# Attention products in row halves and column strips, plain float32, with TensorE's order written out by hand

## The chip, the cores and the metric

The kernel runs on one core of one Trainium2 chip. The metric is the device time of one execution in microseconds. Five engines of the core work side by side, each on its own queue of instructions, in order: PE (TensorE, matrix products, with weight loads shown apart as PEld), DVE (VectorE), ACT (ScalarE), POOL (GpSimd) and SP (SyncE, which issues the DMAs here). They wait for each other through semaphores.

## The reference

A linear attention with exponential features, followed by a gated feed-forward. Sizes: batch 8, 8 heads, 576 positions, head size 64, 128 features; the feed-forward takes 4608 tokens of 512 through 1536 and back. All float32.

```python
def phi(x):
    proj = np.einsum('bhsd,df->bhsf', x, w_phi)
    proj = proj - np.max(np.abs(proj), axis=-1, keepdims=True)
    return np.concatenate([np.exp(proj), np.exp(-proj)], axis=-1)
q_p, k_p = (phi(q), phi(k))
kv = np.einsum('bhsf,bhsd->bhfd', k_p, v)
z = np.sum(k_p, axis=2)
num = np.einsum('bhsf,bhfd->bhsd', q_p, kv)
den = np.einsum('bhsf,bhf->bhs', q_p, z)[..., None] + 1e-06
attn = num / den            # then x: tokens x (heads * head size)
gate = 1.0 / (1.0 + np.exp(-(x @ w_gate)))
val = x @ w_val
out = gate * val @ w_out
```

## The kernel before

**Stages.** The attention goes over 32 pairs: 8 batches of 4 pairs of heads, two heads side by side in 128 partitions. The feed-forward's 1536 inner columns are 12 blocks of 128. Blocks 0 to 4 (`JA = 5`) run beside the attention, in chunks of 256 tokens, as soon as a batch has left its rows in the scratch `xscr`; their partial result goes to `yscr`. After the attention a second phase (`rest_chunks`) runs blocks 5 to 11 in chunks of 512 tokens, adds the partial result and writes the output. The change leaves the second phase as it is.

**A pair.** `att_q` projects q (product `pq`, lines 397 and 403), copies it to `d` and subtracts the largest absolute value, found by DVE over a transposed layout (lines 413 to 428). `att_k` projects k (`pk`, lines 316 and 321), takes maxima (line 325) and exponentials `ek` (line 338 straight from PSUM in the first `DIRECT` = 4 pairs, line 350 after a subtraction in the others), multiplies them with v, which carries a column of ones for the sum z (`kvp`, line 358: v's 65 columns are the weights, 256 features stream), copies the result (`kvt`, line 364) and transposes it in four pieces (`tp`, line 367). `att_num` takes the exponentials of q (`eq`, line 439) and multiplies (`nm`, line 456: 65 columns of weights, the last one the denominator, 288 positions stream). `att_norm` sends the denominator row through DRAM (`dn`, `den`, `rb`) to get reciprocals in all partitions, and `att_scale` multiplies (`xp`, line 484) and writes x.

**Number formats.** A product of plain float32 is two instructions on PE. In the feed-forward and in the attention's projections and numerators from pair 8 on, operands are split into two parts of type float32r (`split`: ACT rounds, DVE takes the rest), and a product becomes three cheaper ones (two for q, where both parts are stacked). The first `WHOLE` = 8 pairs, and `kvp` always, use plain float32.

**Order.** The order of every engine's instructions, PE's included, is worked out by the framework's planner from a simulated timeline and from priorities: attention steps are emitted under `attend` with a priority, and the feed-forward's units are let in by `fill`, called four times a pair, at 0.7 units a call:

```python
due = min(due + RATE, 2.0) if ready else 0.0
while ready and due >= 1.0:
    ready.pop(0)()
    due -= 1.0
```

A unit is a block of a chunk: `mm_in` (line 136) 24 products into `gv`, then `gated`; `half_out` makes the partial result (`mm_out`, line 143, into `acc`). Weights come as float64 words and are taken apart by DVE and ACT (`from_f64`), 15 such pieces while the first pairs run.

**PSUM.** Eight banks: two for `gv`, three for `pp` (pk and pq), one each for `kvp`/`tp`, `nm` and `acc`.

Of the kernel before, what the change touches and what calls it, by code (L numbers as in the profile page):

```python
# [31 lines left out]
KVW = D + 1  # L32
# [3 lines left out]
WHOLE = 8  # first pairs: plain float32 products, no splits  # L36
DIRECT = 4  # first pairs: K's exponentials straight from PSUM
PRIORITY = 400
RATE, LAG = 0.7, 2  # feed-forward units per slot; slots from x to its first unit
# [3 lines left out]
def attention_moe(  # L43
# [29 lines left out]
    def from_f64(h, l, raw, mid, sp, nb, name):  # L73
        # h: the value cut to 12 bits; l: the other bits as an integer times their unit
# [26 lines left out]
    def load_weights(j, m, wp, sp, nb, twice):  # L101
# [58 lines left out]
    def half_units(cs, js, mp, ps_gv, ps_acc):  # L160
# [11 lines left out]
        def unit(c, i):  # L172
            begin(c)
            n = f"1_{c}_{js[i]}"
            gv = ps_gv.tile([P, 2, CH], F32, tag="gv", name="gv" + n)
            for m in range(2):
                mm_in(gv[:, m, :], xs[c], js[i], m, CH)
            hs[c, i] = gated(gv[:, 0, :], gv[:, 1, :], CH, mp, 6, n)
            if i == 1:
                begin(c + 1, hs[c, i][2])  # L180
# [10 lines left out]
        for c in cs:  # L191
            for i in range(len(js)):
                items.append(lambda c=c, i=i: unit(c, i))
                if i == 0:
                    items += outs
            outs = [(lambda c=c, t=t: half_out(c, t)) for t in range(2)]
# [60 lines left out]
    with ExitStack() as actx:  # L257
# [10 lines left out]
        ident = at1.tile([KVW, KVW], F32, name="ident")  # L268
        make_identity(nc, ident)
        wk = at1.tile([P, 3 * F], F32, name="wk")  # L270
        nc.sync.dma_start(wk, w_phi)
        wq = at1.tile([P, 2, 3 * F], F32R, name="wq")
        split(wq[:, 0, :], wq[:, 1, :], wk)
# [3 lines left out]
        loaded, kvs, qst, marks = {}, {}, {}, []  # L277
        rbs, late = {}, {}

        def load_q(b, p):  # L280
            qx = at.tile([P, S], F32, tag="qin", name=f"q{b}_{p}")
            nc.sync.dma_start(qx, q[b, p])
            loaded["q", b, p] = qx

        def load_kv(b, p):
# [3 lines left out]
            vx = at.tile([P, 10, KVW], F32, tag="vin", name="v" + n)  # L289
            nc.sync.dma_start(vx, v[b, p])  # L290
            loaded["kv", b, p] = (kx, vx)

        def att_k(b, p):
            n = f"{b}_{p}"
            kx, vx = loaded.pop(("kv", b, p))
            kvp = ps_kv.tile([KVW, 2, 2 * F], F32, tag="kvp", name="kvp" + n)
            es = []
            whole = b * NP + p < WHOLE
            if not whole:
                kh = at.tile([P, 4 * P], F32R, tag="kh", name="kh" + n, bufs=2)  # L300
                kl = at.tile([P, 4 * P], F32R, tag="kl", name="kl" + n, bufs=2)
                split(kh, kl, kx[:, : 4 * P])
            for g in range(3):
                pp = ps_p.tile([P, 4, F], F32, tag="pp", name=f"pk{n}_{g}")
                if g < 2:
                    ns = 4
                    for i in range(2):
                        o = pp[:, 2 * i : 2 * i + 2, :].rearrange("p a f -> p (a f)")
                        ts = slice((2 * g + i) * P, (2 * g + i + 1) * P)
                        terms = [(kx, wk[:, : 2 * F])] if whole else [  # L310
                            (kh, wq[:, 0, : 2 * F]),
                            (kh, wq[:, 1, : 2 * F]),
                            (kl, wq[:, 0, : 2 * F]),
                        ]
                        for t, (x, w) in enumerate(terms):
                            nc.tensor.matmul(  # L316
                                o, x[:, ts], w, start=t == 0, stop=t == len(terms) - 1
                            )
                else:
                    ns = 1  # L320
                    nc.tensor.matmul(
                        pp[:, 0, :], kx[:, 4 * P :], wk[:, 2 * F :], start=True, stop=True
                    )
                mx = at.tile([P, 4], F32, tag="mx", name=f"mx{n}_{g}")
                vec.tensor_reduce(
                    mx[:, :ns], pp[:, :ns, :], axis=AX.X, op=ALU.max,
                    apply_absolute_value=True,
                )
                e = at.tile(
                    [P, ns, 2 * F], F32, tag=f"ek{ns}", name=f"ek{n}_{g}",  # L330
                    bufs=2 if ns > 1 else 2,
                )
                if b * NP + p < DIRECT:
                    mn = at.tile([P, 4], F32, tag="mn", name=f"mn{n}_{g}")
                    vec.tensor_scalar(mn[:, :ns], mx[:, :ns], -1.0, None, op0=ALU.mult)
                    for i in range(ns):
                        for sg in (1, 0):
                            act.activation(  # L338
                                e[:, i, sg * F : sg * F + F], pp[:, i, :], AF.Exp,
                                bias=(mn, mx)[sg][:, i : i + 1], scale=1.0 - 2.0 * sg,  # L340
                            )
                else:
                    dk = at.tile([P, ns, F], F32, tag=f"dk{ns}", name=f"dk{n}_{g}")
                    vec.tensor_tensor(
                        dk, pp[:, :ns, :],
                        mx[:, :ns].unsqueeze(2).broadcast_to([P, ns, F]),
                        op=ALU.subtract,
                    )
                    for sg in range(2):
                        act.activation(  # L350
                            e[:, :, sg * F : sg * F + F], dk, AF.Exp,
                            scale=1.0 - 2.0 * sg,
                        )
                es.append(e)
            for hd in range(2):
                for t in range(5):
                    slot = 2 * t + hd
                    nc.tensor.matmul(  # L358
                        kvp[:, hd, :], vx[:, slot, :],
                        es[t // 2][:, slot % 4 if t < 4 else 0, :],  # L360
                        start=t == 0, stop=t == 4,
                    )
            kvt = at.tile([KVW, 4, F], F32, tag="kvt", name="kvt" + n, bufs=1)
            act.copy(kvt.rearrange("p a f -> p (a f)"), kvp.rearrange("p a f -> p (a f)"))
            tp = ps_kv.tile([P, 4, KVW], F32, tag="kvp", name="tp" + n)
            for i in range(4):
                nc.tensor.transpose(tp[:, i, :], kvt[:, i, :], ident)
            if b * NP + p < WHOLE:
                kv = at.tile([P, 4, KVW], F32, tag="kv", name="kv" + n)
                act.copy(kv, tp)  # L370
                kvs[b, p] = (kv,)
            else:
                kvh = at.tile([P, 4, KVW], F32R, tag="kv", name="kvh" + n)
                kvl = at.tile([P, 4, KVW], F32R, tag="kvl", name="kvl" + n)
                split(kvh, kvl, tp)
                kvs[b, p] = (kvh, kvl)

        def att_q(b, p):
            n = f"{b}_{p}"
            x = loaded.pop(("q", b, p))  # L380
            early = b * NP + p < WHOLE
            if not early:
                s = at.tile([P, 2, S], F32R, tag="stack", name="sq" + n)
                for hd in range(2):
                    own = slice(hd * D, hd * D + D)
                    oth = slice(D - hd * D, P - hd * D)
                    act.copy(s[own, hd, :], x[own])
# [250 lines left out]
```

## Time and profile before

| what | value |
|---|---|
| median of 3 runs | 1304.17 us (1303.55 to 1304.51) |
| the profiled execution, span | 1307.2 us, 3.0 us over that median |
| granted TensorE clock, mean | 0.992 |
| PE busy | 1269.8 us (97%), 7112 products |
| PE weight loads busy | 1070.8 us (82%) |
| DVE busy | 877.5 us (67%) |
| ACT busy | 650.7 us (50%) |
| POOL busy | 0.6 us |
| DMA | 125.12 MB, 31% of 16 engines |

Records of the profile are the span from the first to the last instruction; the runs' times have no profile, so one profiled execution's own span stands beside them. Products on PE are pipelined: a record is longer than the distance to the next one, so what a product costs in a full queue is read from the distance between starts (the pitch), not from the mean duration. Line numbers are those of the kernel before.

### The profile page before, as it was taken

The numbers are of one execution on the slowest core, as the hardware profiler recorded it, in microseconds if no ns is written. First come the engines' busy times: TensorE is split into PE (matmuls) and PEld (weight loads), VectorE is DVE, ScalarE is ACT, GpSimd is POOL, SyncE is SP. The second block draws the span as 40 slices with busy tenths as digits, with TensorE's granted clock in tenths as the row PEclk, the third lists the DMA queues.
The fourth block names the chain that finished last, engine by engine and source line by source line (L and its number), as shares of the span: only waits on it lengthen the run. The fifth ranks groups of instructions, "written<-read, shape, count | busy, mean of one in ns | idle before, by whom it ended". The sixth has DMA issues, their size and how long they took to land.

```text
span 1307.2 us, 19107 instructions
## 1 busy us (share of the span) xinstructions
PE 1269.8 (97%) x7112; PEld 1070.8 (82%) x7112; DVE 877.5 (67%) x1778; ACT 650.7 (50%) x1416; POOL 0.6 (0%) x6
## 2 busy tenths in 40 slices
PE   7878999999999999999999999999999999999998
PEld 4545788999898989898998988888888888888886
DVE  5777989899899888989866958834343443434333
ACT  5754777777777787777754523322222222222221
POOL 0000000000000000000000000000000000000000
PEclk9988999999999999999999999999999999999999
DMA  5576543233233323332225424313021211202010
GB/s 190 165 216 195 167 131 100 85 107 105 86 115 86 107 84 118 94 108 76 61 69 180 130 78 132 97 65 97 1 97 33 65 50 48 97 1 97 1 65 33
DMA packets 75166, 125.12 MB, mean 96 GB/s; under 512 B 18496, under 2 KB 38080, under 8 KB 75072
## 3 DMA queue, kind: packets, MB, share of 16 engines
q1 hardware_dynamic: 75072, 123.89, 30.7%
q8 instruction: 56, 0.92, 0.3%
q14 instruction: 38, 0.31, 0.1%
HBM read 95.25 MB, written 28.46 MB: 95 GB/s over the span
## 4 chain that ended last, share of the span: by engine, by line
PE 88%; DVE 4%; DMA 4%; ACT 2%; issue 1%; SPq 0%; DVEq 0%; ACTq 0%
PE acc L143 22%; PE gv L136 17%; PE g L136 13%; PE v L136 13%; PE kvp L358 9%; PE nm L456 7%; PE pk L316 3%; PE pq L403 2%; PE pq L397 1%; DMA xs<-xp 1%; DMA q<-q 1%; DMA rb<-den 1%; DMA dn<-ex 1%; ACT ek L338 1%; DMA wraw<-w_moe 1%
## 5 line engine op out<-in xcount | busy, mean ns | idle before, releaser
L136 PE MATMUL gv<-xh,wh 128*128 128x256 f32 x720 | 208.3, 290 | 3.6 <-DVE t L156 3.4
L136 PE MATMUL gv<-xh,wl 128*128 128x256 f32 x720 | 206.5, 287 | 0.0
L136 PE MATMUL gv<-xl,wh 128*128 128x256 f32 x720 | 206.2, 286 | 0.0
L60 ACT CAST hh<-u 128x256 fp32r<-128x256 f32 (+1 forms) x153 | 75.4, 494 | 245.3 <-DVE u L157 245.1
L143 PE MATMUL acc<-wh,hh 128*128 128x512 f32 x432 | 171.3, 397 | 0.7 <-ACT y L187 0.7
L143 PE MATMUL acc<-wl,hh 128*128 128x512 f32 x432 | 169.9, 393 | 0.0
L143 PE MATMUL acc<-wh,hl 128*128 128x512 f32 x432 | 166.1, 394 | 0.1
L358 PE MATMUL kvp<-ek,v 128*65 128x256 f32 x640 | 158.6, 383 | 6.9 <-ACT ek L338 5.3
L155 DVE TENSOR_SCALAR t<-t 128x256 uint32<-128x256 uint32 (+1 forms) x153 | 52.5, 344 | 154.6 <-ACT t L152 153.7
L136 PEld LDWEIGHTS gv<-xh,wh 128*128 128x128 f32 x720 | 137.1, 191 | 10.0 <-DVE t L156 4.7
L136 PEld LDWEIGHTS gv<-xl,wh 128*128 128x128 f32 x720 | 137.0, 190 | 3.3
L136 PEld LDWEIGHTS gv<-xh,wl 128*128 128x128 f32 x720 | 137.0, 190 | 2.3
L358 PEld LDWEIGHTS kvp<-ek,v 128*65 128x65 f32 x640 | 86.6, 138 | 49.4 <-ACT ek L338 9.7
L61 DVE TENSOR_TENSOR hl<-u,hh 128x256 fp32r<-128x256 f32 (+1 forms) x153 | 81.1, 531 | 47.2 <-ACT hh L60 46.1
L152 ACT ACTIVATE t<-g 128x512 f32<-128x512 f32 x63 | 37.6, 597 | 150.0 <-PE g L136 149.8
L156 DVE SCALAR_TENSOR_TENSOR t<-t,v 128x512 f32<-128x512 f32 x63 | 43.3, 687 | 85.6 <-PE v L136 85.4
L136 PE MATMUL g<-xh,wh 128*128 128x512 f32 x252 | 99.0, 393 | 0.0
L136 PE MATMUL v<-xh,wh 128*128 128x512 f32 x252 | 98.6, 391 | 0.0
L136 PE MATMUL g<-xl,wh 128*128 128x512 f32 x252 | 98.6, 391 | 0.0
L136 PE MATMUL g<-xh,wl 128*128 128x512 f32 x252 | 98.5, 391 | 0.0
L136 PE MATMUL v<-xl,wh 128*128 128x512 f32 x252 | 98.3, 390 | 0.0
L136 PE MATMUL v<-xh,wl 128*128 128x512 f32 x252 | 98.2, 390 | 0.0
(91 smaller groups left out, 2533.6 us busy)
## 6 DMA issues: line engine op xcount, KB each, us to landing
wraw<-w_moe SPq DMA_DIRECT2D x36, 512.0 KB, 3.9
xl<-xs SPq DMA_DIRECT2D x36, 512.0 KB, 4.1
v<-v SPq DMA_DIRECT2D x32, 325.0 KB, 3.3
k<-k SPq DMA_DIRECT2D x32, 320.0 KB, 3.1
q<-q SPq DMA_DIRECT2D x32, 288.0 KB, 3.2
rb<-den SPq DMA_DIRECT2D x32, 288.0 KB, 3.8
ys<-y SPq DMA_DIRECT2D x36, 256.0 KB, 2.1
yp<-ys SPq DMA_DIRECT2D x36, 256.0 KB, 4.3
```

What stands on the lines that cost most here:

```text
L60: a = act.copy(h, x)
L61: return a, vec.tensor_tensor(l, x, h.bitcast(F32), op=ALU.subtract)
L136: nc.tensor.matmul(o, a[:, ws], x[:, cs], start=i == 0, stop=i == 11)
L143: nc.tensor.matmul(acc, a[:, ts], w[:, ws], start=first and i == 0, stop=last and i == 2)
L152: act.activation(t, g, AF.Tanh, scale=0.5)
L155: vec.tensor_scalar(tu, tu, 0x7FFFFFFF, None, op0=ALU.bitwise_and)
L156: vec.scalar_tensor_tensor(t, t, 1.0, vl, op0=ALU.add, op1=ALU.mult)
L316: nc.tensor.matmul(o, x[:, ts], w, start=t == 0, stop=t == len(terms) - 1)
L338: act.activation(e[:, i, sg * F : sg * F + F], pp[:, i, :], AF.Exp, bias=(mn, mx)[sg][:, i : i + 1], scale=1.0 - 2.0 * sg,)
L358: nc.tensor.matmul(kvp[:, hd, :], vx[:, slot, :], es[t // 2][:, slot % 4 if t < 4 else 0, :], start=t == 0, stop=t == 4,)
L403: nc.tensor.matmul(pp, wq[:, i, 2 * F :], s[:, hd, cs], start=i == 0, stop=i == 1,)
L456: nc.tensor.matmul(nm, a[:, 2 * hd + sg, :], x[:, hd, :], start=sg == 0 and i == 0, stop=sg == 1 and i == last,)
```

## The change

The attention is written anew; the feed-forward's arithmetic stays.

- **Everything in the attention is plain float32.** The splits of k, q, kv and the exponentials go, with `wq`, `kh`, `kl`, `sq`, `eqh`, `eql`, `kvh`, `kvl`.
- **Row halves.** The projections of q and k no longer stream both heads against weights padded with zeros. A head lies in 64 partitions, and its products use those 64 rows of the array; the two heads alternate (`q_half`, `k_heads`).
- **Column strips.** `kv` and `num` have weights of 32 columns (`Q = 32`) and give each product its strip by `tile_position=(0, o)`; four strips of one bank follow one another. v loses its column of ones. Instead POOL adds the exponentials of k over the positions in a partition (`su`), a product with 32 columns of ones gives the sums z replicated in 32 rows, three 128 x 128 transposes (`turn`) replace four smaller ones, and the denominators are products of their own (`dp`).
- **PSUM.** The three pools of the attention become one of five banks in rotation (`ps_a`).
- **PE's order by hand.** `tc.manual_schedule` for PE: PE runs its instructions in the order in which the program emits them; the other engines are still planned. The loop works two pairs at once: q and k of pair i + 1, kv and transposes of pair i, and from pair `EARLY + 1` = 5 on the numerators of pair i - 1. Feed-forward units are cut in halves (gate, value) with a cost each and spread over `SPOTS` = 16 calls of `fill`.
- **DMAs.** Loads are asked for two pairs ahead; the denominator goes out in four pieces and comes back in two; `xp` is one multiplication over 128 partitions.

The diff, cut to its core:

```diff
+    ctx.enter_context(tc.manual_schedule(engines={mybir.EngineType.PE}))
-        ps_p = actx.enter_context(tc.tile_pool(name="ps_p", bufs=3, space=PSUM))
-        ps_kv = actx.enter_context(tc.tile_pool(name="ps_kv", bufs=1, space=PSUM))
-        ps_n = actx.enter_context(tc.tile_pool(name="ps_n", bufs=1, space=PSUM))
+        ps_a = actx.enter_context(tc.tile_pool(name="ps_a", bufs=5, space=PSUM))
+        def q_half(i, hf):
...
+            pps = [bank([P, HS], f"pq{n}{hd}") for hd in range(2)]
+            for hd in range(2):
+                nc.tensor.matmul(
+                    pps[hd], wk[head(hd), :], x[head(hd), cs], start=True, stop=True
+                )
+            for hd in range(2):
+                act.copy(d[:, hd, cs], pps[hd])
+        def k_heads(i):
+            kx = loaded["k", i]
+            pps = [bank([P, 4, F], f"pk{i}_{hd}") for hd in range(2)]
+            for t in range(4):
+                for hd in range(2):
                     nc.tensor.matmul(
+                        pps[hd][:, t, :], kx[head(hd), t * P : t * P + P],
+                        wk[head(hd), :], start=True, stop=True,
                     )
+            for hd in range(2):
+                k_exp(i, hd, pps[hd], 4)
+        def k_rest(i):
...
+            for hd in range(2):
+                pool.tensor_tensor(su[:, hd, :], es[hd][:, 0, :], es[hd][:, 1, :], op=ALU.add)
+                for t in (2, 3):
+                    pool.tensor_tensor(su[:, hd, :], su[:, hd, :], es[hd][:, t, :], op=ALU.add)
+            for hd in range(2):
+                pool.tensor_tensor(
+                    su[head(hd), hd, :], su[head(hd), hd, :], es[2][head(hd), 0, :],
+                    op=ALU.add,
+                )
+        def kv(i):
...
+            kvz = bank([P, 3 * F], f"kvz{i}")
+            for t in range(5):
+                for o in range(0, P, Q):
+                    hd = o // D
+                    nc.tensor.matmul(
+                        kvz[o : o + Q, : 2 * F],
+                        vx[:, 2 * t + hd, o % D : o % D + Q],
+                        (e0, e1)[hd][:, t, :] if t < 4 else e2[:, 0, :],
+                        start=t == 0, stop=t == 4, tile_position=(0, o),
+                    )
+            for o in range(0, P, Q):
+                hd, sg = divmod(o // Q, 2)
+                nc.tensor.matmul(
+                    kvz[o : o + Q, 2 * F :], ones, su[:, hd, sg * F : sg * F + F],
+                    start=True, stop=True, tile_position=(0, o),
+                )
+            kvt = at.tile([P, 3 * F], F32, tag="kvt", name=f"kvt{i}", bufs=1)
+            act.copy(kvt, kvz)
+        def turn(i):
...
+            for m in range(3):
+                nc.tensor.transpose(tp[:, m, :], kvt[:, m * F : m * F + F], ident)
+            kvs[i] = at.tile([P, 3, P], F32, tag="kv", name=f"kv{i}")
+            act.copy(kvs[i], tp)
+        def q_exp(i):
...
+                e = at.tile([P, 2, S], F32, tag=f"eq{sg}", name=f"eq{i}_{sg}", bufs=1)
+                act.activation(e, d, AF.Exp, scale=1.0 - 2.0 * sg)
+        def num(i):
...
+            for hf in range(2):
+                cs = slice(hf * HS, hf * HS + HS)
+                for sg in range(2):
+                    for o in range(0, P, Q):
+                        nc.tensor.matmul(
+                            nms[hf][o : o + Q, :], w[:, sg, o : o + Q],
+                            es[sg][:, o // D, cs],
+                            start=sg == 0, stop=sg == 1, tile_position=(0, o),
+                        )
+            for sg in range(2):
+                for o in range(0, P, Q):
+                    hd, hf = divmod(o // Q, 2)
+                    z = (2 * hd + sg) * Q
+                    nc.tensor.matmul(
+                        dp[o : o + Q, :], w[:, 2, z : z + Q],
+                        es[sg][:, hd, hf * HS : hf * HS + HS],
+                        start=sg == 0, stop=sg == 1, tile_position=(0, o),
                     )
+        def norm(i):
...
+            for o in range(0, P, Q):
+                nc.sync.dma_start(dn[o : o + Q, :], dr[o : o + 1, :])
...
+            for hd in range(2):
                 nc.sync.dma_start(
+                    rb[head(hd), :], dens[i][hd].unsqueeze(0).broadcast_to([D, S])
                 )
+            due += sum(c for c, _ in ready) / max(1, SPOTS - since)
+            while ready and due >= ready[0][0] / 2:
+                cost, f = ready.pop(0)
+                f()
+                due -= cost
+        for i in range(-1, N + 1):
...
+            if i + 2 < N:
+                attend(load_q, i + 2)
+                attend(load_kv, i + 2)
+            if i + 1 < N:
+                attend(q_half, i + 1, 0)
+                attend(k_heads, i + 1)
+                fill()
+                attend(q_half, i + 1, 1)
+                attend(k_rest, i + 1)
+                attend(q_max, i + 1)
+                fill()
+            if i >= EARLY + 1:
+                attend(q_exp, i - 1)
+            if 0 <= i < N:
+                attend(kv, i)
+            if i >= EARLY + 1:
+                attend(num, i - 1)
             fill()
+            if 0 <= i < N:
+                attend(turn, i)
+            if i >= EARLY + 1:
+                finish(i - 1)
             fill()
+            if 0 <= i < EARLY:
+                attend(q_exp, i)
+                attend(num, i)
+                finish(i)
```

`finish` is `norm`, then `scale`, and after the fourth pair of a batch `queue`, which puts the batch's chunks on the list three spots (`LAG`) later.

More of the change, by code (lines that the diff above doesn't have):

```diff
@@ L170, in begin, with half @@
                 xs[c] = xh, xl
-        def unit(c, i):
+        gvs, accs = {}, {}
+        def half(c, i, m):
             begin(c)
             n = f"1_{c}_{js[i]}"
[L175 to L180, printed above, removed]
+            if m == 0:
+                gvs[c, i] = ps_gv.tile([P, 2, CH], F32, tag="gv", name="gv" + n)
+            gv = gvs[c, i]
+            mm_in(gv[:, m, :], xs[c], js[i], m, CH)
+            if m == 1:
+                hs[c, i] = gated(gv[:, 0, :], gv[:, 1, :], CH, mp, 6, n)
+                if i == 1:
+                    begin(c + 1, hs[c, i][2])
         def half_out(c, t):
@@ L192, in half_units @@
             for i in range(len(js)):
-                items.append(lambda c=c, i=i: unit(c, i))
+                for m in range(2):
+                    items.append((1.45, lambda c=c, i=i, m=m: half(c, i, m)))
                 if i == 0:
                     items += outs
-            outs = [(lambda c=c, t=t: half_out(c, t)) for t in range(2)]
+            outs = [(0.69 * len(js), lambda c=c, t=t: half_out(c, t)) for t in range(2)]
         return items + outs
@@ L276, in attention_moe, with head, load_q, load_kv @@
         ]
-        loaded, kvs, qst, marks = {}, {}, {}, []
-        rbs, late = {}, {}
-        def load_q(b, p):
+        steps = [(b, p) for b in range(B) for p in range(NP)]
+        loaded, ks, ds, kvs, marks, rbs = {}, {}, {}, {}, [], {}
+        def head(hd):
+            return slice(hd * D, hd * D + D)
+        def load_q(i):
+            b, p = steps[i]
             qx = at.tile([P, S], F32, tag="qin", name=f"q{b}_{p}")
             nc.sync.dma_start(qx, q[b, p])
-            loaded["q", b, p] = qx
-        def load_kv(b, p):
+            loaded["q", i] = qx
+        def load_kv(i):
+            b, p = steps[i]
             n = f"{b}_{p}"
@@ L288, in load_kv @@
             nc.sync.dma_start(kx, k[b, p])
-            vx = at.tile([P, 10, KVW], F32, tag="vin", name="v" + n)
+            vx = at.tile([P, 10, D], F32, tag="vin", name="v" + n)
             nc.sync.dma_start(vx, v[b, p])
[L291 to L320, printed above, removed]
@@ L354, in att_k @@
[L354 to L364, printed above, removed]
@@ L365, in att_k @@
[L365 to L376, printed above, removed]
@@ new lines, in num @@
+        def num(i):
+            es, w = ds.pop(i), kvs.pop(i)
+            ex = at.tile([P, S], F32, tag="ex", name=f"ex{i}")
+            nms = [bank([P, HS], f"nm{i}_{hf}") for hf in range(2)]
+            dp = bank([P, HS], f"dp{i}")
+            for hf in range(2):
+                cs = slice(hf * HS, hf * HS + HS)
+                for sg in range(2):
[4 more added lines that the diff above has]
+                            start=sg == 0, stop=sg == 1, tile_position=(0, o),
+                        )
+            for sg in range(2):
+                for o in range(0, P, Q):
[5 more added lines that the diff above has]
+                        start=sg == 0, stop=sg == 1, tile_position=(0, o),
+                    )
+            dr = at.tile([P, HS], F32, tag="dr", name=f"dr{i}", bufs=1)
+            act.copy(dr, dp)
+            for hf in range(2):
+                act.copy(ex[:, hf * HS : hf * HS + HS], nms[hf])
+            rbs[i] = (ex, dr)
@@ L496, in attention_moe @@
         js = list(range(JA))
-        steps = [(b, p) for b in range(B) for p in range(NP)]
-        load_q(*steps[0])
-        load_kv(*steps[0])
         ready, coming = [], []
-        cdone = wdone = slot = 0
+        cdone = wdone = spot = since = 0
         due = 0.0
         def fill():
-            nonlocal due, slot
-            slot += 1
-            while coming and coming[0][0] <= slot:
+            nonlocal due, spot, since
+            spot += 1
+            since += 1
+            while coming and coming[0][0] <= spot:
                 ready.extend(coming.pop(0)[1])
-            due = min(due + RATE, 2.0) if ready else 0.0
-            while ready and due >= 1.0:
-                ready.pop(0)()
-                due -= 1.0
-        def attend(f, *a):
-            with tc.high_priority(offset=PRIORITY):
-                f(*a)
+                since = 0
+            if not ready:
+                due = 0.0
+                return
+            due += sum(c for c, _ in ready) / max(1, SPOTS - since)
[3 more added lines that the diff above has]
+                due -= cost
         def queue(b):
@@ L549, in attention_moe @@
                 wdone += 1
-            fill()
-            if i and p == 0:
-                queue(b - 1)
-        attend(att_norm, *steps[-1])
-        attend(att_scale, *steps[-1])
-        queue(B - 1)
         for _, x in coming:
             ready.extend(x)
-        for f in ready:
+        for _, f in ready:
             f()
```

244 lines of the change are left out of this document (94 added, 150 removed).

## The prediction

> **What bounds the kernel now.** I read the page's head, then the busy table by stretches, then the chain of work that ended last, for the stage beside the attention.
>
> ```profile
> span 1307.2 us, 19107 instructions
> 0.00:116.00 116.00, 90.93 (x362) 56.66 (x362) 82.11 (x188) 68.32 (x180) 0.60 (x6) 0.93 0.59 189
> 116.00:665.00 549.00, 545.18 (x3697) 483.37 (x3697) 487.91 (x1030) 402.38 (x914) 0.00 (x0) 1.00 0.36 104
> 665.00:785.00 120.00, 117.26 (x802) 107.46 (x801) 82.63 (x196) 51.61 (x116) 0.00 (x0) 1.00 0.36 117
> 785.00:1307.00 522.00, 516.39 (x2257) 423.28 (x2255) 224.89 (x365) 128.37 (x207) 0.00 (x0) 1.00 0.19 61
> by line: PE gv L136 33.7%; PE kvp L358 20.1%; PE acc L143 16.6%; PE nm L456 14.4%; PE pk L316 6.5%; PE pq L403 4.9%; PE tp L367 1.1%; PE pk L321 1.0%; issue 0.6%; DVE dk L344 0.3%; DVE kl L61 0.2%; DVE pn L422 0.1%; DVE t L156 0.1%; DVE eql
> ```
>
> The columns of a stretch are its length, then busy time on PE, weight loads, DVE, ACT, POOL, the granted clock and the DMA share. From 116 us (the first feed-forward product) to 665 us (the last attention products) PE works 545.2 of 549 us at clock 1.00, while DVE (488) and ACT (402) have room. The last line is the chain inside 220 to 640 us: 98% of it is PE. So in this stage time is PE's queue, and a product is worth its pitch there. Before 116 us no feed-forward work exists yet, PE is busy 91 of 116 us, at clock 0.93. After 785 us nothing changes.
>
> The pitch of each kind comes from runs in the chain (time, length, count) and from rows of the timeline:
>
> ```profile
> 747.47 5.75 PE gv L136 x48
> 1287.62 2.77 PE acc L143 x12
> 228.22 3.45 PE kvp L358 x16
> 425.02 0.80 PE nm L456 x6
> 300.82 1.44 PE pk L316 x12
> 425.83 0.80 PE pq L403 x6
> 65.54 0.97 PE nm L456 x4
> 67.00 1.73 PE pk L316 x8
> 22.94 0.41 PE L367 MATMUL tp<-ident,kvt 65*128 65x65 f32 x4
> L358 PE MATMUL kvp<-ek,v 128*65 128x256 f32 x640 | 158.6, 383 | 6.9 <-ACT ek L338 5.3
> L321 PE MATMUL pk<-wk,k 128*128 128x128 f32 x64 | 12.5, 277 | 0.0
> ```
>
> Feed-forward: 5.75/48 = 120 ns for 256 columns, 231 ns for 512. Plain float32 stands as two instructions: kvp is 320 products and 640 records, 216 ns each; pk whole 1.73/8 = 216 ns; nm whole (288 columns) 0.97/4 = 243 ns. Split products: nm 133, pk 120, pq 133 ns. The four transposes lie (0.41 - 0.224)/3 = 62 ns apart, 0.224 being their mean duration; that is the shortest spacing of a load with its product I found. A product of 128 columns in float32 has about half of 216, 109 ns. The excess of kvp's duration over its pitch, 383 - 216 = 167 ns, is what a product takes after its columns have gone in.
>
> **The change, part by part.**
>
> *Attention on PE, before.* A split pair (24 of 32): kvp 20 x 0.216 = 4.32, nm 24 x 0.133 = 3.19, pk 12 x 0.12 + 2 x 0.109 = 1.66, pq 8 x 0.133 = 1.06, tp 0.25: 10.5 us. The chain's own shares give 48.0% of 420 us, 201.6 us:
>
> ```profile
> L428 DVE TENSOR_TENSOR d<-d,mb x32: 1339/1354/1360, 14.3 to 656.3; 128x1152 f32<-128x1152 f32 x32
> ```
>
> One subtraction per pair, so 642/31 = 20.7 us a pair, 20.3 pairs in 420 us, 9.9 us each. I take 10.2. A whole pair (first 8, of which 3 run beside the feed-forward) is 4.32 + 16 x 0.243 + 1.73 + 0.22 + 8 x 0.243 + 0.25 = 12.4; taken 12.2. Of 32 pairs, 27 pay in full on PE's queue; the first five run before 116 us.
>
> *Attention on PE, after.* All plain float32. Instructions a pair (two a product): q 8 in two row halves, k 8 x 2 in row halves, the rest of k 2, kv 5 x 4 x 2 = 40 and its sums 8 in four column strips, num 32 and denominators 16 in strips, three transposes. No row of before shows two products at once, so bounds. If each runs alone: 8 x 0.243 + 18 x 0.109 + 40 x 0.216 + 8 x 0.109 + 48 x 0.243 + 0.37 = 25.5 us, the upper end. If the halves run two at a time and the strips four at a time: q 0.97, k 0.87 + 0.22, kv 2.16 + 0.22, num and denominators 2.92, transposes 0.37 (three of twice the columns at 2 x 62 ns): 7.7 us, the lower end. In between stands issue: the 96 strip instructions at 62 ns are 5.95 us instead of 5.3; those 62 ns belong to loads of 128 columns, a strip loads 32, so I take half way, 5.6, and 8.0 for the pair. I take the four-at-a-time end because consecutive products go to disjoint strips of columns and write disjoint partitions, so nothing in the data makes one wait for the next.
>
> PE now also goes from whole array to halves to strips and back, six times a pair. Bounds: 0, or a full 167 ns each, 1.0 us; I take 0.4, since a neighbour's loads can go ahead as they do now. So 8.4 us (7.7 to 9.4).
> Saved: 24 x (10.2 - 8.4) + 3 x (12.2 - 8.4) = 43 + 11 = **54 us** (27 to 74).
>
> The Trainium skill, "TensorE: Matmul & The Clock Gate", Part 3, has three column strips at 2.38 times one, 79% of ideal. By that the strips' 5.3 us would be 6.7 us, the pair 9.5 us, the saving 25 us and the time about 1283; an estimate from that page, no run here shows it yet.
>
> *Work taken from DVE and ACT.*
>
> ```profile
> L447 DVE TENSOR_TENSOR eql<-eq,eqh 128x576 fp32r<-128x576 f32 x96 | 70.2, 752 | 11.0 <-ACT eqh L446 9.6 <-PE pq L403 1.2
> L446 ACT CAST eqh<-eq 128x576 fp32r<-128x576 f32 x96 | 60.7, 671 | 37.7 <-PE nm L456 37.7
> L388 DVE TENSOR_TENSOR sq<-q,sq 64x576 fp32r<-64x576 f32 x48 | 36.1, 753 | 1.5
> L387 ACT CAST sq<-q 64x576 fp32r<-64x576 f32 x48 | 32.1, 668 | 0.6
> L484 DVE TENSOR_TENSOR xp<-ex,rb 64x576 f32<-64x576 f32 x64 | 47.9, 749 | 10.9 <-DMA rb<-den 10.4
> L157 DVE SCALAR_TENSOR_TENSOR u<-u,t 128x256 f32<-128x256 f32 x90 | 37.6, 420 | 1.2
> ```
>
> DVE loses 70 + 36 + half of xp, 24 = 130 us, ACT 93 us. Neither was the bound, so 0 on the path; they keep 358 and 309 us in a stage of some 500, and if PE came under 11 us a pair beside the attention's, DVE would be next. POOL gets eight additions of 256 columns a pair. No row of POOL is like that; DVE's 256-column row is 420 ns, so 3.4 us, at three times that 10 us. They are ready a whole iteration (some 19 us) before kv needs them: 0 until POOL passes 15 us a pair.
>
> *PE's order by hand.* What a product waits for now holds up everything behind it on PE: the transposes wait for ACT's copy of kvz, which num and a slice of feed-forward cover (2.9 + about 3 us against a 0.6 us copy); kv waits for a bank of PSUM that DVE frees after maxima and differences (2.7 us of DVE, covered by two slices). Bounds 0 and 25 us (1 us a pair); I take **+6**.
>
> *DMAs.* Denominators go out in four pieces instead of two and come back in two instead of one: three issues more a pair on SP, which has long waits of its own and delays no one here. Loads are asked for two pairs ahead; v's buffer is freed only by kv of the same iteration, so SP stands there until then, and behind it are the denominators of the pair before, which PE makes after that kv anyway, and the feed-forward's x, asked for three spots ahead: 0.
>
> *The start.* The chain of the first 116 us:
>
> ```profile
> by line: PE kvp L358 12.2%; PE pq L397 11.0%; PE nm L456 7.2%; DMA q<-q 7.0%; issue 6.6%; ACT ek L338 5.7%; DMA xs<-xp 5.5%; DMA wmid<-w_moe 4.5%; DMA dn<-ex 4.3%; ACT eq L439 4.1%; DMA rb<-den 3.1%; PE pk L316 3.0%; DMA xl<-xs 2.9%; DVE mx
> ```
>
> PE is 33% of it, 39 us; cut by 7.7/12.4 that is 15 us less at the best, and q's waits (7%) may go as well: 0 to -20. DVE's 82 us stay, and the first feed-forward spot is now fixed in PE's order behind pair 5's q and k. I take **-8**.
>
> *The end.* The last pair's result goes through DMAs before its feed-forward work can begin:
>
> ```profile
> 91.83 5.00 DMA dn<-ex
> 98.60 1.51 DMA den<-dn
> 100.13 3.63 DMA rb<-den
> 103.78 0.75 DVE xp L484
> 105.32 6.42 DMA xs<-xp
> 111.76 3.32 DMA xl<-xs
> ```
>
> That is the same chain at the first batch, 24 us to 116 us. At the end, before had feed-forward work left over (PE 117 of 120 us busy after 665 us). After spreads a batch over 16 spots, and the last two iterations have two spots fewer each, so a quarter of a batch of 42 us (two chunks of 120 x 0.12 + 30 x 0.231 us), 10.6 us, is left to cover some 17 us: **+6** (0 to 10).
>
> **Sum.** 1307.2 - 54 - 8 + 6 + 6 = 1257.2 us for a profiled execution. The median shown is 1304.17, 3.0 us under the profiled span, so **1254 us**. With all ends good 1307 - 74 - 20 - 3 = 1210; all bad 1307 - 27 + 10 + 25 - 3 = 1312.
>
> **Rivals.**
>
> *Two at a time (slower).* The two halves of a float32 product stand next to each other in PE's queue:
>
> ```profile
> 511.73 0.48 PE L403 MATMUL pq<-sq,wq 128*128 128x288 f32 x1
> 512.05 0.60 PE L358 MATMUL kvp<-ek,v 128*65 128x256 f32 x2
> 512.29 0.48 PE L403 MATMUL pq<-sq,wq 128*128 128x288 f32 x1
> ```
>
> kvp comes as x2 between single pq. Both halves need the same strip, so the second waits for the first; if PE starts products strictly in order, the next strip's first half can only start with that second half, and each product costs one pitch however many strips there are. Then q and k stay as forecast, kv is 20 x 0.216 + 4 x 0.109 = 4.76, num and denominators 24 x 0.243 = 5.83, the pair 13.4 us with the switches: 24 x 3.2 + 3 x 1.2 = 80 us more, and 1307 + 80 + 4 - 3 = **1388 us**. It decides as soon as the mean overlap in strips is below about 2.9: one at a time they are 21.2 us, and above 7.4 us nothing is saved. For it: starts follow the program in every stretch of before I looked at. Against: that stream never offers another strip. The Trainium skill, "TensorE: Matmul & The Clock Gate", Part 3, says products keep strict order in start and end, which is this rival's premise; the examples it gives have no second half.
>
> *No overlap at all.* 25.5 + 0.4 us a pair: 27 pairs 415 us more and some 30 in the start, about **1750**. Nothing in the trace excludes it, but distinct columns speak against it.
>
> *The order by hand eats it.* Products as forecast, but DVE gives the banks of k's products back late: PE waits 2 us a pair, 54 us, in the place of the 54 saved: about **1302**, no change; beyond that slower. Against it: DVE falls from 488 to 358 us of work.
>
> **Chances.** Four at a time 0.60 (own range 1210 to 1312), two at a time 0.23, the order by hand 0.10, no overlap 0.04, something faster than 1210 0.03. The range must leave out no more than 2 in 10, so it reaches over two at a time: 1212 to 1392. A measurement tells 0.2% (2.6 us) from no change. Faster by that: most of the 0.60, the 0.03 and a little of the third, 0.63; within it 0.04; slower 0.33.
>
> **What would show it.** Right: records of kvz, nm and dp overlap four deep, a group of eight strip instructions spans about 0.45 us, PE's attention is 8 to 9 us of an 18.5 us pair, attention ends near 600 us. Wrong: strip products start 216 ns apart (two at a time), or PE idles before kvz or tp with DVE or ACT as releaser (the order), or PE is idle over 10 us ahead of the last batch.

## The result and the profile after

The changed kernel takes 1405.48 us (median of 4, 1404.1 to 1407.21) against 1304.34 us for the kernel before on the same chip: a ratio of 1.0769, 95% interval 1.0754 to 1.0784. It is slower by 101 us; 1254 us was forecast, and the time lies above the range's upper end of 1392 us.

The page's head, then busy time by stretches of the kernel after (length, PE, weight loads, DVE, ACT, POOL, granted clock, DMA share, GB/s). The cuts are the first feed-forward product (133 us), the last attention product with what is left beside it (780 us) and the start of the second phase (880 us):

```profile
span 1405.4 us, 22696 instructions
PE 1249.7 (89%) x8968; PEld 990.2 (70%) x8968; DVE 778.8 (55%) x1554; ACT 535.4 (38%) x1151; POOL 208.4 (15%) x262
0.00:133.00 133.00, 66.38 (x601) 35.38 (x601) 97.88 (x190) 61.23 (x154) 40.80 (x54) 0.74 0.57 183
133.00:780.00 647.00, 579.85 (x5591) 454.03 (x5592) 388.46 (x841) 310.47 (x713) 167.55 (x208) 0.93 0.28 88
780.00:880.00 100.00, 83.99 (x512) 75.27 (x511) 66.03 (x156) 35.06 (x77) 0.00 (x0) 0.91 0.36 117
880.00:1405.00 525.00, 519.52 (x2269) 425.48 (x2267) 226.43 (x369) 128.62 (x208) 0.00 (x0) 1.00 0.19 62
```

The same cuts in the kernel before:

```profile
116.00:687.00 571.00, 567.18 (x3859) 504.40 (x3859) 499.79 (x1056) 413.87 (x941) 0.00 (x0) 1.00 0.35 103
687.00:782.00 95.00, 92.26 (x627) 83.98 (x626) 68.74 (x166) 39.52 (x88) 0.00 (x0) 1.00 0.39 127
782.00:1307.00 525.00, 519.39 (x2270) 425.73 (x2268) 226.90 (x370) 128.96 (x208) 0.00 (x0) 1.00 0.19 62
```

The start is 17 us longer, the stage beside the attention 76 us, its tail 5 us, the second phase the same: 98 us. PE's busy time fell by 20 us (1269.8 to 1249.7), and its idle time rose by 118 us, from 37 to 156. Of these 156 us, 67 lie in the start, where the kernel before had 25, and 67 in the stage beside the attention, where it had 4. Each stretch with stops also runs at a lower granted clock, 0.74, 0.93 and 0.91. The longer start holds less work, too: by 133 us PE has done kv of five pairs and the numerators of four, where the kernel before had done kv of six and the numerators of five and a half by 116 us.

The products themselves did nearly what they were forecast to do. One pair's strips in PE's timeline (start, length, count), and the transposes of two pairs that follow one another without a stop at clock 1.00:

```profile
396.16 0.28 PE L137 MATMUL gv<-xh,wl 128*128 128x256 f32 x1
396.37 2.37 PE L414 MATMUL kvz<-ek,v 128*32 128x256 f32 x40
398.55 0.40 PE L422 MATMUL kvz<-su,ones 128*32 128x128 f32 x8
398.77 2.12 PE L456 MATMUL nm<-eq,kv 128*32 128x288 f32 x32
400.71 1.16 PE L465 MATMUL dp<-eq,kv 128*32 128x288 f32 x16
401.79 0.39 PE L137 MATMUL gv<-xh,wh 128*128 128x256 f32 x1
402.02 0.28 PE L137 MATMUL gv<-xl,wh 128*128 128x256 f32 x1
642.43 0.49 PE L434 MATMUL tp<-ident,kvt 128*128 128x128 f32 x3
661.30 0.49 PE L434 MATMUL tp<-ident,kvt 128*128 128x128 f32 x3
```

From the first kvz to the next gv are 5.42 us for 96 instructions that would take 21.2 us one at a time: four run at once (in the trace four start within 20 ns, the next four 216 or 243 ns later). From one pair's transposes to the next are 18.87 us; 84 feed-forward products at the pitch of 120 ns are 10.1 us of it, so a pair of attention with its switches takes 8.8 us, where 8.4 was forecast. A switch between whole array and strips costs 0.09 us: kvz starts 0.21 us after the gv before it, where one gv follows another after 0.12.

What PE waited for (engine, tile and line, releaser: total, times, longest):

```profile
PE gv L137 <- ACT xh L61: 56.8, 8, 20.1
PE tp L434 <- ACT kvt L427: 18.2, 6, 7.6
PE gv L137 <- DVE t L157: 17.5, 8, 3.7
PE acc L144 <- ACT hh L61: 15.8, 6, 4.7
PE nm L456 <- ACT kv L436: 10.7, 4, 5.8
PE pq L315 <- DMA wk<-w_phi: 9.3, 1, 9.3
```

The largest is, in seven of its eight cases, a batch's first feed-forward product: in PE's written order it stands three spots after its batch, and x has not come through the DMAs. PE then starts nothing of what stands behind it. The first two batches make 35.5 of the 56.8 us. For the second:

```profile
217.79 1.15 PE L465 MATMUL dp<-eq,kv 128*32 128x288 f32 x16
239.75 0.58 PE L137 MATMUL gv<-xh,wh 128*128 128x256 f32 x1 [15.40 <-ACT xh L61]
```

From the end of the batch's last denominators to its first feed-forward product are 20.8 us. The three spots in between had no feed-forward work left to let in, so PE had only transposes and q and k of one pair there, some 4 us of work.

And the feed-forward became dearer after such stops. Here is one stop of 2.05 us, with no other over 0.15 us in the few us before it; 0.8 us later the products get longer. The last line is the stretch of 3.4 us that follows, its columns as above, with a granted clock of 0.50:

```profile
555.13 0.39 PE L137 MATMUL gv<-xh,wh 128*128 128x256 f32 x1 [2.05 <-DVE t L157]
555.98 0.42 PE L137 MATMUL gv<-xh,wh 128*128 128x256 f32 x1
555.90:559.30 3.40, 3.40 (x28) 2.26 (x31) 3.27 (x12) 1.19 (x4) 0.00 (x0) 0.50 0.62 195
```

Over the whole kernel (busy time, mean in ns, idle time before):

```profile
L137 PE MATMUL gv<-xh,wh 128*128 128x256 f32 x720 | 221.3, 307 | 74.8 <-ACT xh L61 56.8
L137 PE MATMUL gv<-xl,wh 128*128 128x256 f32 x720 | 213.4, 296 | 5.0 <-DVE xl L62 5.0
L137 PE MATMUL gv<-xh,wl 128*128 128x256 f32 x720 | 212.0, 294 | 0.0
```

Against 208.3, 206.2 and 206.5 before that is 26 us, and the three acc groups add 9 (175.1 + 170.4 + 171.1 against 171.3 + 166.1 + 169.9). These 35 us are the half clock's: 200 of the 2160 gv products lie in pieces of half clock and have a median of 415 ns, the others 283 as in the kernel before; with 25 acc products of 628 instead of 390 ns that makes 34.5 us. So the 20 us that PE is busy less are about 55 us saved in the attention, over all 32 pairs, and 35 us lost in the feed-forward's same products.

### The profile page after: what moved, and what is told of

Same layout as the page of the kernel before. It is cut to its first block, busy times and chain, and to the rows that moved or that the text cites. A ratio compares the mean times of both kernels' runs of the same rounds, so it can differ in the third digit from the quotient of the medians.

```text
span 1405.4 us, 22696 instructions
## 1 busy us (share of the span) xinstructions
PE 1249.7 (89%) x8968; PEld 990.2 (70%) x8968; DVE 778.8 (55%) x1554; ACT 535.4 (38%) x1151; POOL 208.4 (15%) x262
## 4 chain that ended last, share of the span: by engine, by line
PE 65%; DMA 12%; DVE 11%; ACT 6%; issue 3%; SPq 2%; DVEq 0%; ACTq 0%
PE acc L144 18%; PE gv L137 13%; PE g L137 12%; PE v L137 12%; PE kvz L414 3%; DMA rb<-den 3%; DMA xl<-xs 3%; PE nm L456 2%; PE pq L315 2%; DMA den<-dn 1%; DMA dn<-dr 1%; ACT ek L346 1%; ACT eq L443 1%; SPq L481 1%; PE dp L465 1%
## 5 line engine op out<-in xcount | busy, mean ns | idle before, releaser
L137 PE MATMUL gv<-xh,wh 128*128 128x256 f32 x720 | 221.3, 307 | 74.8 <-ACT xh L61 56.8
L137 PE MATMUL gv<-xl,wh 128*128 128x256 f32 x720 | 213.4, 296 | 5.0 <-DVE xl L62 5.0
L137 PE MATMUL gv<-xh,wl 128*128 128x256 f32 x720 | 212.0, 294 | 0.0
L137 PEld LDWEIGHTS gv<-xh,wh 128*128 128x128 f32 x720 | 146.0, 203 | 91.5 <-ACT xh L61 58.4
L144 PE MATMUL acc<-wh,hh 128*128 128x512 f32 x432 | 175.1, 405 | 21.6 <-ACT hh L61 15.8
L144 PE MATMUL acc<-wh,hl 128*128 128x512 f32 x432 | 170.4, 394 | 1.7 <-DVE hl L62 1.7
L144 PE MATMUL acc<-wl,hh 128*128 128x512 f32 x432 | 171.1, 396 | 0.0
L137 PEld LDWEIGHTS gv<-xl,wh 128*128 128x128 f32 x720 | 146.6, 204 | 7.1 <-DVE xl L62 7.0
L137 PEld LDWEIGHTS gv<-xh,wl 128*128 128x128 f32 x720 | 146.8, 204 | 0.0
L372 POOL TENSOR_TENSOR su<-ek 128x256 f32<-128x256 f32 x64 | 59.0, 922 | 537.1 <-ACT ek L346 449.1
L144 PEld LDWEIGHTS acc<-wh,hh 128*128 128x128 f32 x432 | 82.4, 191 | 45.7 <-ACT hh L61 18.6
L346 ACT ACTIVATE ek<-dk 128x512 f32<-128x512 f32 (+1 forms) x168 | 75.4, 513 | 73.8 <-DVE dk L340 53.8
L374 POOL TENSOR_TENSOR su<-su,ek 128x256 f32<-128x256 f32 x128 | 102.9, 813 | 3.5
```

The costliest lines, as they stand in the source:

```text
L137: nc.tensor.matmul(o, a[:, ws], x[:, cs], start=i == 0, stop=i == 11)
L144: nc.tensor.matmul(acc, a[:, ts], w[:, ws], start=first and i == 0, stop=last and i == 2)
L346: act.activation(e[:, :, sg * F : sg * F + F], dk, AF.Exp, scale=1.0 - 2.0 * sg)
L372: pool.tensor_tensor(su[:, hd, :], es[hd][:, 0, :], es[hd][:, 1, :], op=ALU.add)
L374: pool.tensor_tensor(su[:, hd, :], su[:, hd, :], es[hd][:, t, :], op=ALU.add)
```

## The experiments

**Order back to the planner; hand order for the old products.** Theory A: the hand-written order is the loss. Theory B: the strips are.

```diff
-    ctx.enter_context(tc.manual_schedule(engines={mybir.EngineType.PE}))
```

> The kernel after, only without the manual schedule: PE's order comes from the planner again, all else as it is. Theory A (the hand-written order is the loss: PE idles 118 us more than before and runs some 57 us of products at half clock after those stops): PE's idle time falls from 156 to 40 to 70 us and the time to 1260 to 1310 us, if the planner keeps the four strips together. Theory B (the strips themselves are the loss: they slow the clock and the feed-forward's products beside them): the idle time moves, the slow clock stays, the time stays at 1380 us or more.

1509.45 us, ratio 1.1571 (1.1541 to 1.1601): slower still. It lies in theory B's range (1380 us or more), but not for B's reason: the granted clock rose from 0.939 to 0.968. Theory A's condition, strips kept together, did not hold. PE idles less (75 us) but is busy 1431 us:

```profile
span 1505.6 us, 22723 instructions
PE 1431.0 (95%) x8968; PEld 1049.9 (70%) x8968; DVE 789.0 (52%) x1554; ACT 542.1 (36%) x1151; POOL 203.9 (14%) x262
394.79 0.67 PE L455 MATMUL nm<-eq,kv 128*32 128x288 f32 x2
395.30 0.59 PE L413 MATMUL kvz<-ek,v 128*32 128x256 f32 x2
395.83 0.50 PE L144 MATMUL acc<-wh,hh 128*128 128x512 f32 x1
396.26 0.67 PE L455 MATMUL nm<-eq,kv 128*32 128x288 f32 x2
```

In such stretches the planner deals single products of nm and kvz (x2, two instructions) in turn with instructions of acc, 1.47 us a round. Strips pay when four stand together, so this change needs some order by hand; the run does not say what this hand order costs. The same line put into the kernel before:

```diff
+    ctx.enter_context(tc.manual_schedule(engines={mybir.EngineType.PE}))
```

> The kernel before, only with the manual schedule for PE: its own products in the order in which its program emits them. Theory A: PE stands at every hand-over, since the program emits kvp right behind pk and the numerators right behind the transposes; 5 to 10 us a pair, 1450 to 1600 us. Theory B: the order matters little where products are cheap and whole, 1304 to 1330 us.

1681.2 us (one run): theory A's side, above its range. The old program, emitted pair by pair, does not serve as PE's order as it is.

**A batch's feed-forward one pair later.**

```diff
-LAG = 3
+LAG = 7
```

> The kernel after with LAG = 7 instead of 3: a batch's first feed-forward unit stands four spots (one pair, some 20 us) later in PE's order, behind another pair's attention. Theory A: the 57 us that PE waits for xh, the rounded x of a batch, go to under 10, with them some 10 us of half clock; the first batch starts a pair later and costs up to 15 us of that: 1340 to 1365 us. Theory B: 1395 to 1410 us, and the clock in the stage stays under 0.95.

1368.8 us, 1.0485 (1.0467 to 1.0502), 37 us less than the kernel after, where theory A had 1340 to 1365. PE's wait for xh fell from 56.8 to 3.6 us, but other waits grew:

```profile
PE acc L144 <- ACT hh L61: 26.8, 8, 6.9
PE tp L434 <- ACT kvt L427: 24.6, 9, 8.0
```

**Strips one after another.** The loops over strips go outside:

```diff
-            for t in range(5):
-                for o in range(0, P, Q):
+            for o in range(0, P, Q):
+                for t in range(5):
```

and likewise in `num` and the denominators.

> The kernel after with the loops over strips turned inside out in kv, num and the denominators: all products of one strip follow one another, then the next strip's. Same products, same banks. If PE starts products strictly in the order of its queue, a strip's products run one after another and only the seams overlap: the strips' 5.5 to 6 us a pair become some 20 us, 32 pairs, part of it hidden in what PE idles now: 1750 to 1900 us. If each strip has a queue of its own, nothing changes: 1400 to 1410 us. The prediction's rival of two at a time would follow from strict order with the two halves of a product side by side.

1489.89 us (one run): between the two. kv's 40 instructions take 6.3 us from the first start to the last end (409.50 to 415.82 us) instead of 2.4:

```profile
409.50 5.67 PE L414 MATMUL kvz<-ek,v 128*32 128x256 f32 x37
414.80 0.42 PE L422 MATMUL kvz<-su,ones 128*32 128x128 f32 x6
415.23 0.46 PE L456 MATMUL nm<-eq,kv 128*32 128x288 f32 x3
415.44 0.38 PE L414 MATMUL kvz<-ek,v 128*32 128x256 f32 x1
```

nm, which stands behind all of kv in PE's order, starts at 415.23, before kvz's last instruction at 415.44. The trace does not name strips, but its starts fit the second strip setting in 1.32 us after the first, with the seventh of the first strip's ten instructions. So a product can pass others that wait for their strip, but only a few, and "in order", as the first section has it, is not strict on PE. That is enough for four strips in turn, and not enough for ten in a row on one strip.

**Smoothing the waits.** Rival C: the waits move. In e5 `LAG` is 5, and a batch's last output products are held until the next batch's first unit is issued:

```diff
+            items, outs = half_units(cs, js, moe, ps_gv, ps_acc)
+            coming.append((spot + LAG, items[:2] + held + items[2:]))
+            held[:] = outs
```

> The kernel after with LAG = 5 and with the output products of a batch's last chunk held back until the next batch's first unit has been issued, so that they no longer stand right behind the gate and value products whose result they need. With LAG = 7 alone PE waited 27 us for hh at those places and 4 us for xh. Theory A (each wait in PE's order costs its length and some clock): hh under 5 us, xh under 15 us, 1335 to 1355 us. Rival C (the waits only move: the time is set by the rate at which DVE, ACT and the DMAs deliver a pair): the idle time turns up before other products, 1360 to 1375 us.

```diff
-EARLY = 4
+EARLY = 0
```

> The kernel of e5_carry with EARLY = 0: the numerators of the first four pairs too come an iteration later, so that num of the pair before stands between kv and its transposes. Theory A: PE's waits for kvt and kv in the first 130 us (34 us with LAG = 7) fall to 10 to 20 us, 1320 to 1345 us. Rival C: the first pairs are paced by ACT and DVE; the first feed-forward product starts no sooner and the time is that of e5_carry within 8 us.

```diff
+        with tc.high_priority(offset=2 * PRIORITY):
             nc.sync.dma_start(wk, w_phi)
```

> The kernel of e6_early0 with the 64 KB of w_phi asked for first instead of behind six loads of 288 to 320 KB on SP. PE's first product started at 9.3 us in the kernel after and at 4.2 us in the kernel before. Theory A: 4 to 5 us less than e6_early0. Rival C: the first pair waits for its k and v anyway, 0 to 1 us less.

1377.78 us (1.0531 to 1.0572 of before), 1365.64 (1.0399 to 1.0482) and 1360.0 (1.0391 to 1.0436). e5 gained nothing over LAG = 7 (it lost 9 us): hh fell to 3.6 us, xh came back at 19 us with LAG = 5, and a new wait of 18.8 us stood before kvz. e6 is 12 us under e5, above theory A's range and more than rival C allowed. e7's first product starts at 4.2 us instead of 9.5; its time is 6 us under e6, but the two intervals overlap, so that gain is not sure. Rival C had the mechanism of e5 right, with a time 3 us above its range. Where a stop comes from is seen on DVE, here in e5 (in brackets: idle before it, and its releaser):

```profile
367.41 0.49 PE L366 MATMUL pk<-wk,k 128*128 128x128 f32 x2
370.23 0.76 DVE L495 TENSOR_TENSOR xp<-ex,rb 128x576 f32<-128x576 f32 x1 [1.79 <-DMA rb<-den]
370.91 1.28 DVE L340 TENSOR_TENSOR dk<-pk,mx 128x512 f32<-128x512 f32 x2
371.70 2.79 PE L414 MATMUL kvz<-ek,v 128*32 128x256 f32 x24 [3.80 <-issue]
```

DVE stands at xp for the DMA; behind it is dk, which frees the bank of PSUM that kvz takes next; PE starts kvz 0.15 us after the first of the two dk is done. The profile itself names no releaser there ("issue"). This is theory C: DVE and ACT stand at the head of their queues for a DMA, and PE, in a fixed order, stands with them.

```diff
+            with tc.issue_after(marks[-1].ins):
                 vec.tensor_tensor(xp, ex, rb, op=ALU.mult)
```

> The kernel of e7_wk with one edge more: the multiplication xp = ex * rb, which waits for a DMA, is queued on DVE behind the latest q_max instead of where the planner put it, ahead of dk, the subtraction that frees k's banks of PSUM. In e7_wk DVE stood 72 us at xp and PE 18 us before kvz, each time right after xp. Theory C (PE's waits come from DVE and ACT standing at the head of their queues for a DMA): DVE's wait at xp falls under 25 us, PE's stops before kvz under 5 us, 1335 to 1350 us. Theory A (only PE's own order): 1358 to 1362 us.

1364.5 us (1.0426 to 1.0484): a miss. The edge binds xp behind an instruction that stood before it already; DVE's wait at xp stayed at 74.9 us, PE's before kvz at 19.0 us. In the trace DVE's order is the same as in e7: xp still stands ahead of the next pair's dk. So e8 does not test theory C.

```diff
-                    behind(stack, marks)
+                    behind(stack, [*marks, *amarks[-1:]])
...
-            attend(norm, i)
             attend(scale, i)
...
+            if i >= 2:
+                finish(i - 2)
...
-                finish(i - 1)
+                attend(norm, i - 1)
```

That is the core of it: `norm` stays behind the numerators, its reciprocals go behind q's latest subtraction, `scale` comes one pair later (with two buffers for `rb`), and x is rounded behind q's latest copy. In the same run `LAG` is 3 again, and the output products held back are spread out.

> The kernel of e8_xp with the other waits for DMAs moved back in the same way: the reciprocals behind the latest q_max, the multiplication one pair later (two buffers for rb), the rounding of a chunk's x on ACT behind the latest copy of q, LAG = 3 counted from there, and the two output products of a chunk separated by a half unit. Theory C: ACT's wait for x (61 us) and DVE's for dn and rb fall by more than half, PE's idle time from 117 to 60 to 80 us, 1290 to 1325 us. Theory A: PE's idle time stays above 100 us, 1345 us or more.

1327.63 us, 1.0170 (1.0142 to 1.0198): 37 us less than e8, just above theory C's range; PE's idle time is 94 us (1330.5 - 1236.3) where 60 to 80 was expected. The waits before kvz of e5 are gone, and DVE's at xp went from 75 to 10.5 us, but its wait at dn rose from 50 to 72: together they fell by a third, not by half. Several changes came at once, so the run does not say what each of them won:

```profile
DVE dn L485 <- DMA dn<-dr: 72.4, 23, 6.8
DVE xp L499 <- DMA rb<-den: 10.5, 3, 5.8
```

**Later still.** e10: the feed-forward one spot later, three for the first batch. e11: the reciprocals half a pair and xp a pair later.

```diff
-            coming.append((spot + LAG, items[:3] + ...
+            coming.append((spot + LAG + (3 if b == 0 else 1), items[:3] + ...
```

> The kernel of e9_behind with the first batch's feed-forward work three spots later and every other batch's one spot later in PE's order. e9_behind still waits 24 us for xh, 15 us of it at the first batch, where PE then stands although another pair's attention is ready. Theory C: that wait under 6 us, half of it won because the first pairs are paced by DVE anyway: 1308 to 1322 us. Theory A: the same. Rival D (the first 130 us are set by DVE's own work, whatever PE's order): 1322 to 1330 us.

```diff
+            if i >= 3:
+                finish(i - 3)
...
+            if i >= 2:
+                attend(recip, i - 2)
```

Here `recip` is the reciprocals, cut out of `norm`, and `scale` (in `finish`) now stands behind k's latest subtraction on DVE.

> The kernel of e10_lag with the reciprocals of the denominators half a pair later and the multiplication xp a pair later on DVE, behind k's subtraction, so that DVE reaches both after their DMAs have landed. In e9_behind DVE stood 72 us at dn. Theory C: DVE's waits at dn and xp together under 25 us, PE's idle time 15 to 30 us less than e10_lag, 1285 to 1310 us; at the lower end it beats the kernel before. Theory A (DVE's waits don't reach PE): the time of e10_lag within 5 us.

1317.6 us (1.0070 to 1.0126), inside the range that theories A and C shared, and 1311.07 us (ratio 1.0046, 1.0030 to 1.0062). With DVE's wait at dn gone and 21.5 us left at xp, PE's idle time fell from 82 to 77 us, less than the 15 us expected; e11 lies 1 us above theory C's range and, 6.5 us under e10, 1.5 us outside theory A's; it does not beat the kernel before. Its stretches, cut as above:

```profile
0.00:146.00 146.00, 99.59 (x978) 56.74 (x979) 125.76 (x234) 81.47 (x202) 55.37 (x74) 0.78 0.59 190
146.00:660.00 514.00, 498.16 (x4981) 394.08 (x4980) 362.73 (x769) 280.51 (x639) 159.69 (x189) 0.98 0.32 100
660.00:785.00 125.00, 115.97 (x747) 107.10 (x746) 77.37 (x186) 45.93 (x104) 0.00 (x0) 0.95 0.34 111
```

From the first feed-forward product to the second phase it takes 639 us against before's 666. The start takes 30 us more, 146 against 116, with DVE busy 126 us of it. The 27 us are not all a gain, since part of it is work done sooner: kv of eight pairs and the numerators of seven lie before 146 us, against six and five and a half before 116 us in the kernel before.

**The start.**

```diff
+            if 2 <= i < NP + 2:
+                finish(i - 2)
+            if i >= NP + 2:
+                attend(recip, i - 2)
...
+                if i <= NP:
+                    attend(recip, i - 1)
```

> The kernel of e11_recip, but the first four pairs take the short way of e10_lag (reciprocals in their own pair, the multiplication one pair later), since the first feed-forward product came at 146 us in e11_recip, 130 us in e10_lag and 116 us before. If PE is short of work until then, as theory C has it, 8 to 14 us less than e11_recip: 1297 to 1304 us, level with the kernel before or just under it. Rival D (the first stage is set by DVE, and attention done early there is work saved later): 1308 to 1314 us.

1313.38 us, 1.0061 (1.0048 to 1.0075): rival D's range. The first feed-forward product starts at 129.6 us instead of 145.6, with one pair less of attention done, and the time is that of e11 within the intervals. Hurrying the first batch out wins nothing here, which fits rival D: attention done early is work saved later. That DVE's pace sets the first stage fits too, but no run gave DVE less to do there.

## Why the prediction was wrong

- **Products, 54 us saved:** right in mechanism, a little too large. Four ran at once: 5.42 us of strips (5.6 forecast), 8.8 us a pair (8.4 forecast). By the prediction's own sum that saves 24 x 1.4 + 3 x 3.4 = 44 us.
- **Two at a time, the rival at 1388 us:** did not happen; that its time is the nearest to the result is chance. Its premise was strict order. Here four strips ran four deep with two instructions a product, and with the loops turned round (e4) nm started 0.21 us ahead of kvz's last instruction, which stands before it in PE's order: a few may be passed. The Trainium skill, "TensorE: Matmul & The Clock Gate", Part 3, states that products keep strict order in start and end; the trace does not agree, and the measurement decides. By three strips at 2.38 times one, from the same part of that page of the Trainium skill, the strips were estimated at 6.7 us; the trace has 5.42.
- **PE's order by hand, +6 us (0 to 25):** the step that failed. PE idles 118 us more than before. The step looked at copies on ACT and at banks freed by DVE, and found cover for each. The hand-over of x to a batch's first feed-forward product it left out, and under DMAs x was put at 0 because it is asked for three spots ahead. But x goes through the same chain of DMAs that the prediction quoted for the end (24 us there), once a batch, and three spots of some 18.5 us a pair are 14 us at most; behind the second batch they held 4 us of work. That wait alone is 56.8 us, and 37 us of time in e3. The step also did not see that the planner could now place DVE's and ACT's waits for DMAs ahead of work that PE needs.
- **Half clock:** not in the sum at all. It cost about 35 us in the feed-forward's unchanged products. It follows the stops: the granted clock is 1.00 in stretches that PE fills and 0.74 to 0.93 where PE stands, and the trace's pieces of half clock, mostly 3.4, 6.8 or 10.2 us long, each lie at or behind stops of PE. The Trainium skill, "TensorE: Matmul & The Clock Gate", Part 1, has the clock fall back to half after an idle window of some 3.4 us; the trace agrees in kind, but not in length: the stop of 2.05 us at 553 us was enough.
- **Order by hand as a rival at 1302 us:** right in kind, PE's order ate the saving, but not in its mechanism. Banks of k's products late from DVE are not among the kernel's larger waits; they showed only in e5, as 18.8 us before kvz. Its price was far too small.
- **Start, -8 us:** wrong in sign, +17. PE's busy time there did shrink, from 91 to 66 us, but DVE is busy 98 of 133 us, the first product waited 9.3 us for w_phi behind six larger loads on SP (which the working passed over; moving it forward won at most some 6 us in e7), and 20 us went at the first hand-over of x.
- **End, +6:** the tail is 5 us longer.

Shown by runs: the strips' cost and depth; that the planner's order, which breaks them up, is slower still; that a later hand-over of x wins 37 us (e3); and that with the same products the time comes down to 1311 us by order and waits alone (e3 to e11), so that the strips themselves are not the loss. Of that, e9 won 37 us with several changes at once, e10's later feed-forward 10 us, and e11's moved waits on DVE 7 us. Only read from traces: that the stops cause the half clock, since no run changed the clock alone. Open: what each change in e9 is worth, and what a start with less work on DVE could give; no version here is faster than the kernel before.

## What to carry to other kernels

When one engine's order is fixed by hand, a wait of another engine for a DMA can become a wait of that engine: list each hand-over through DRAM, count its chain in the trace, and give it that much work in the fixed order. Make sure that this work exists: spots are no cover when nothing is left to put into them. Products in column strips of float32 ran four at a time here where four strips stood together. And price a new stop on PE at more than its length: what runs after it can run at half clock.

## What was not expected of the hardware

- PE passes waiting products of one strip with a few of another: ten in a row on one strip leave kv at 6.3 us, where 40 pitches of 0.216 and the last product's 0.167 would be 8.8.
- DVE's subtraction of two operands in SBUF is slower beside POOL's additions. In the kernel after:

```profile
L404 DVE TENSOR_TENSOR d<-d,mb x32: 1336/1359/1891, 24.7 to 751.5; 128x1152 f32<-128x1152 f32 x32
L374 POOL TENSOR_TENSOR su<-su,ek x128: 712/732/1933, 16.0 to 755.9; 128x256 f32<-128x256 f32 x128
```

Minimum, median, maximum in ns; before, the same subtraction was 1339/1354/1360. Of the 32, the 17 that have POOL's additions beside them for at least nine tenths of their time have a median of 1727 ns, the 14 that touch none 1357. POOL takes 732 ns for 256 columns, where DVE's nearest row had 420.
